# Sums of unmasked banks three units behind their exponentials, and the stretches' limits chosen anew

## The chip, the cores and the metric

The kernel runs on one core of a Trainium2 chip. The time is the device's, in microseconds, from the start of the program to its end; three executions were timed, and one more was profiled. The engines are TensorE (PE, with its weight loads as PEld), VectorE (DVE), ScalarE (ACT), GpSimd (POOL) and SyncE (SP), which issues the DMAs. Each engine works its own list of instructions in order, and semaphores hold one back until another has got far enough.

## The reference

Four layers stand one after the other, on 2048 tokens with 512 features; each adds its result to x.

```python
x = x + _A_ref(_layernorm(x), A_wq, A_wk, A_wv, A_wo, A_beta)   # layer 0
x = x + _B_ref(_layernorm(x), B_wqkv, B_wo)                     # layer 1
x = x + _A_ref(...)                                             # layer 2
x = x + _B_ref(...)                                             # layer 3
```

Layer A has 32 heads of 16 features and four segments of 512 tokens. In a segment it is causal attention (softmax of q·k / 4 under a mask), mixed by a gate for each head with a memory: `num / den`, where `num = phi(q) @ M`, `den = phi(q) @ z`, and `M`, `z` are summed over `phi(k)` and `v` of the segments before. Layer B is plain attention of all 2048 tokens with all, 32 heads, no mask. Both end in a product with `wo`. Nothing in the change touches what is computed.

## The kernel before

A **bank** is one PSUM bank of 128 keys x 512 queries of scores of one head (PSUM has eight). Layer A has masked banks (`k0`, `k13`, `k2`), layer B unmasked ones. A **group** is one head pair's half for one segment of queries: the banks whose exponentials are summed into one sums bank. For each bank three things happen: TensorE makes the scores (`ps<-qm,KB` or `ps<-qm,KA`), an exponential is taken, and TensorE multiplies it with V, extended by a column of ones, which gives numerator and denominator (`pv`, `pv_mm`; these are the "sums").

The exponential has two ways. ACT takes it from PSUM into the ring `pT` (line 1925): two or three banks of a **unit** in one instruction. Or DVE takes it: it turns the scores of a bank into the bits of a bf16 power of two (`dx_first`, line 1394, 16 bits a number), and two shifted copies of those (lines 1450 and 1493 on DVE, line 1475 on POOL, in `task_dx`, `dx_four`, `pool_copy`) are summed with the first, so a bank on DVE costs three products with V in place of one. A unit has three banks for ACT, or two for ACT and one or two for DVE.

The order of all engines' instructions is made by a planner in Python when the program is built (class `Sched` with modelled times, `Builder.attention`). For each unit n it puts into the lists: the scores (`unit`), ACT's exponential, some background work (layer norms, projections, output products, memory; `background`, `bg_one`), and then the sums that are due (`pv_step`). `unit` appends its banks to a first-in, first-out queue `pvq` with the unit in which their sums are due:

```python
entries.append((n + (self.LAG_A if g.kind == "A" else 2), g, what, r, slot, i, width))
```

`pT` has `NPU = 4` slots, used in turn, so what is still queued from unit n-4 is forced out before the exponential of unit n is put down. When a group's last sums are out, `finish` has DVE empty the sums bank (lines 2037 and 2043 for a masked group, line 759 or 2068 to 2072 for an unmasked one, which is written as `ub` in its last part). The next group takes that bank, or the spare one if that comes free earlier (`take_sums`). While the sums bank is late, `attention` puts off the sums of a new group until they are forced.

Whether a bank goes to DVE is decided unit by unit (`dx_open`, `ring_open`, `dx_pick`) by limits, among them: `TAKEN`, the share of a group's banks that DVE may take (`TAKEN_A`, banks of a masked group); `PAIRS`, how many banks must lie ahead for pairs; `PACE`, after how many units without a background task DVE's banks stand back; `POOL_D` and `POOL_C`, how far POOL may be behind DVE and still take the first and the second copy; `FILL` and `keep_busy`, below which share of TensorE's activity products of zeros are put in. The units are cut into 76 **stretches** of 20, and the dictionary `PLAN` gives the limits of each stretch where they differ from the class's own values (`set_limits`). Since each stretch starts from the state that the ones before it left, other limits in one place shift what stands in all later stretches.

Of the kernel before, what the change touches and what calls it, by code (L numbers as in the profile page):

```python
# [416 lines left out]
class Builder:  # L417
# [3 lines left out]
        0: dict(TAKEN_A=1, FILL_DVE=400, MASK_PE=800, PE_LOW=7, GAP=3, QMIN=3, OPART=0, DIV_LATE=2500, PACE=2, DX_LATE=1700, HURRY=1500, POOL_QM=1, POOL_C=0, CR_A=1200, CR_LOW=2000),  # L421
        1: dict(ACT1=300, MARGIN=600, R_LATE=2200, NEAR=5, CR_W=1300, CR_B=1800, R_PAIRS=2, DIV_LATE=2500, TAKEN=0.5, DVE_LATE=800, BG_BANK=100, PHI_LATE=300, OPART=3, NEARW=20, POOL_C=0, DX_LAG=1, POOL_D=2500, REST=8, EARLY=500, POOL_QM=1, DX_FIN=3000, DMA_LATE=1200, TRADE=400, FILL_DVE=400, ORD=13, PACE=12, DMA_STEPS=2, HOLD_AT=12, PE_B=2, TAKEN_A=1, MASK_PE=800, PE_LOW=7, PE_A=4, POOL_MEM=0),
        2: dict(FILL_DVE=400, MASK_PE=800, GAP=3, BG_BANK=400, QMIN=3, LOW=20, POOL_QM=1, ACT1=600, R_PAIRS=2, PE_LOW=7, DX_LATE=1700, DX_FIN=3000, OPART=3, HOLD_AT=12, PE_A=4, NEAR_A=50, TRADE=0, TAKEN_A=1, PART=3, DMA_LATE=700, CR_B=1200, SLACK=350, DMA_STEPS=0, POOL_WAIT=600, MARGIN=250, EVAC_ACT=1500),
# [3 lines left out]
        6: dict(ACT1=300, NEAR=8, TAKEN_A=1, PV_SKIP=900, FILL_DVE=400, BACK=8, CR_W=2200, NEARW=40, OPART=0, TAKEN=0.4, LOW=20, DVE_LATE=800, QWAIT=8, HOLD_AT=40, PHI_LATE=0, REST=20, POOL_D=2500, R_LATE=1200, MARGIN=350, EARLY=300, QUAD=0, CR_A=1700, CARRY_W=1500, PART=3, BUSY_WAIT=500, PE_LOW=7, PE_A=6, HURRY=4000, PAIRS=999, LEVEL=3, DX_BANK=900, DX_LATE=700, QMIN=3, TRADE=400, DVE_LATE_LOW=2500, PACE=7, DVE_FIN=1500, MASK_PE=800, FILL=0.47, DMA_LATE=0),  # L427
        7: dict(R_LATE=1200, NEARW=40, PAIRS=999, MASK_PE=800, LEVEL=3, TAKEN=0.4, LOW=20, MARGIN=350, TAKEN_A=1, EARLY=300, OPART=0, QUAD=0, FILL=0.47, DX_BANK=900, CR_A=1200, DX_LATE=700, CARRY_W=400, PART=3, CR_W=2200, HOLD_MAX=0, DVE_LATE=800, FILL_DVE=400, BUSY_WAIT=500, ACT1=300, DMA_LATE=0, GAP=3, QWAIT=8, NEAR=8, PE_A=6, POOL_QM=1, DVE_LATE_LOW=2500, PACE=7, DVE_FIN=200, HURRY=1500, PV_SKIP=900, POOL_D=2500, PE_LOW=7, QMIN=3),
        8: dict(R_LATE=1200, NEARW=40, PAIRS=999, MASK_PE=800, LEVEL=3, TAKEN=0.4, LOW=30, MARGIN=500, TAKEN_A=1, EARLY=500, OPART=0, QUAD=0, FILL=0.47, DX_BANK=900, CR_A=1200, DX_LATE=700, CARRY_W=1500, PART=3, CR_W=2200, DVE_LATE=1700, FILL_DVE=400, BUSY_WAIT=500, ACT1=300, DMA_LATE=0, QWAIT=8, NEAR=8, PV_SKIP=900, NEAR_A=0, HURRY=1500, QMIN=3),
# [66 lines left out]
        75: dict(DX_LATE=500, REST=8, SLACK=700, R_NEAR=10, R_PAIRS=2, NEARW=90, PAIRS=999, LEVEL=1, LOW=14, GAP=1, QUAD=0, POOL_WAIT=300, PV_SKIP=100, BACK=6, FILL=0.47, PART=0, LN1_AT=3, EARLY=300, DIV_LATE=2500, MARGIN=350, POOL_C=1000, ACT1=300, MASK_PE=200, POOL_D=1200, BUSY_ROOM=300, CR_W=1500, TAKEN=0.5, CR_A=1700, CR_LOW=2000, DX_BANK=700, RATE=2, QWAIT=3, DVE_FIN=1500, POOL_QM=1, DMA_LATE=0),  # L496
# [36 lines left out]
    RUSH, RUSH0 = 0, 0  # L533
# [1832 lines left out]
```

## Time and profile before

| what | us |
|---|---|
| timed executions | 1660.08, 1661.16, 1660.99 (median 1660.99) |
| the profiled execution | 1660.92 |
| its span, first to last instruction | 1659.2 |
| ACT busy | 1622.0 (98%) |
| PE busy | 1573.7 (95%) |
| DVE busy | 1397.2 (84%) |
| POOL busy | 1227.6 (74%) |

PE's busy time is that of pipelined matmuls, and its ends are modelled. A row of a group reads: line, engine, operation, what is written and read, shape, count, then busy time and the mean of one instruction in ns, then the engine's idle time ahead of them and what ended it. A row of the windows reads: from and to, length, then busy time (count) of PE, PEld, DVE, ACT and POOL, the granted clock, DMA share and GB/s; where one line or tile was asked for, only its engine stands there. A row of waits has the total in us, how often, and the longest.

### The profile page before, as it was taken

How to read it: one execution, taken by the hardware profiler on the slowest of the kernel's cores; microseconds unless marked ns; L12 is line 12 of the kernel's file. 1: busy time of each engine (PE TensorE's matmuls, PEld its weight loads, DVE VectorE, ACT ScalarE, POOL GpSimd, SP SyncE). 2: the span in 40 equal slices, each digit the busy share in tenths (PEclk: the TensorE clock that was granted, in tenths of full speed). 3: DMA queues.
4: the chain of work that ended last, by engine and by line, in shares of the span. 5: the costliest groups of instructions: out<-in, count | busy, mean ns of one | idle time of the engine just before them, and what ended most of it. 6: DMA issues, size and time to landing. Idle time of an engine off the chain costs nothing.

```text
span 1659.2 us, 45418 instructions
## 1 busy us (share of the span) xinstructions
PE 1573.7 (95%) x19667; PEld 568.6 (34%) x19738; DVE 1397.2 (84%) x2232; ACT 1622.0 (98%) x1575; POOL 1227.6 (74%) x1322
## 2 busy tenths in 40 slices
PE   8999999999999999999999999999999999999998
PEld 5553435222222535222235222442222222222236
DVE  5668666979998687899878997779899999999996
ACT  7999999999999999999999999999999999999998
POOL 3342234779898443699875898577899999999995
PEclk9999999999999999999999999999999999999999
DMA  6211211001120322200212102112001200100000
GB/s 185 41 21 26 40 27 28 8 8 30 23 62 11 72 68 43 58 11 14 58 24 31 49 14 55 18 21 53 1 14 24 46 11 11 27 11 11 22 16 19
DMA packets 148424, 54.46 MB, mean 33 GB/s; under 512 B 128768, under 2 KB 147712, under 8 KB 148224
## 3 DMA queue, kind: packets, MB, share of 16 engines
q1 hardware_dynamic: 148224, 51.56, 14.8%
q8 instruction: 154, 2.52, 0.7%
q14 instruction: 46, 0.38, 0.1%
HBM read 18.88 MB, written 2.10 MB: 13 GB/s over the span
## 4 chain that ended last, share of the span: by engine, by line
ACT 60%; PE 25%; DVE 9%; DMA 2%; POOL 2%; issue 1%; SPq 0%; ACTq 0%; POOLq 0%
ACT pT L1925 59%; PE ps L683 24%; DVE KA L1394 2%; DVE dxt L1394 1%; ACT amem L966 1%; DVE wA L1394 1%; DVE wB L1394 1%; DMA tb<-ub 1%; DMA xT<-xn 1%; DMA phq<-amem 1%; DMA phk<-KA 0%; SPq L766 0%; POOL pT L1939 0%; DVE lnst L873 0%; DVE xn L895 0%
## 5 line engine op out<-in xcount | busy, mean ns | idle before, releaser
L1925 ACT ACTIVATE pT<-ps 128x1024 bf16<-128x1024 f32 (+1 forms) x1503 | 1592.0, 1230 | 21.0 <-PE ps L683 18.1
L683 PE MATMUL ps<-qm,KB 32*128 32x512 bf16 x4096 | 543.9, 385 | 53.3 <-ACT pT L1925 39.0
L683 PE MATMUL ps<-pT,VB 128*17 128x512 bf16 x2751 | 476.7, 384 | 1.6 <-DVE dxt L1394 0.7
L1475 POOL TENSOR_TENSOR dxt<-dxt,shift 128x512 int32<-128x512 int32 (+1 forms) x293 | 312.8, 1079 | 103.2 <-DVE dxt L1394 73.3
L1394 DVE TENSOR_SCALAR KA<-ps 128x512 uint16<-128x512 f32 (+1 forms) x438 | 339.3, 793 | 24.1 <-PE ps L683 21.7
L683 PEld LDWEIGHTS ps<-qm,KB 32*128 32x128 bf16 x4096 | 139.4, 91 | 558.7 <-ACT pT L1925 442.5
L1394 DVE TENSOR_SCALAR dxt<-ps 128x512 uint16<-128x512 f32 (+1 forms) x332 | 257.3, 789 | 27.3 <-PE ps L683 25.7
L1475 POOL TENSOR_TENSOR QA<-KA,shift 128x512 int32<-128x512 int32 x208 | 227.3, 1103 | 53.4 <-DVE KA L1394 52.9
L683 PE MATMUL ps<-dxt,VB 128*17 128x512 bf16 x1125 | 249.8, 381 | 0.3 <-POOL dxt L1475 0.3
L683 PEld LDWEIGHTS ps<-pT,VB 128*17 128x17 bf16 x2751 | 111.0, 87 | 272.8 <-issue 257.4
L1475 POOL TENSOR_TENSOR VA<-KA,shift 128x512 int32<-128x512 int32 x172 | 184.7, 1083 | 24.0 <-DVE QA L1450 18.5
L1939 POOL TENSOR_SCALAR_AFFINE_SELECT pT<-pT 128x512 bf16<-128x512 bf16 (+4 forms) x135 | 71.7, 546 | 170.7 <-ACT pT L1925 170.4
L1475 POOL TENSOR_TENSOR wA<-wA,shift 128x512 int32<-128x512 int32 (+1 forms) x140 | 151.8, 1096 | 9.8 <-DVE wA L1394 6.4
L683 PE MATMUL ps<-QA,VB 128*17 128x512 bf16 x499 | 145.6, 381 | 0.0
L683 PE MATMUL ps<-VA,VB 128*17 128x512 bf16 x499 | 143.6, 381 | 0.0
L1475 POOL TENSOR_TENSOR wB<-wB,shift 128x512 int32<-128x512 int32 x114 | 124.0, 1102 | 5.9 <-DVE wB L1394 4.3
L683 PE MATMUL ps<-KA,VB 128*17 128x512 bf16 x499 | 127.6, 381 | 0.0
L1394 DVE TENSOR_SCALAR wA<-ps 128x512 uint16<-128x512 f32 (+1 forms) x150 | 120.6, 817 | 8.2 <-PE ps L683 7.3
L683 PE MATMUL ps<-wA,VB 128*17 128x512 bf16 x558 | 125.4, 381 | 0.0
L1394 DVE TENSOR_SCALAR wB<-ps 128x512 uint16<-128x512 f32 (+1 forms) x128 | 103.7, 823 | 4.9 <-PE ps L683 4.7
L683 PE MATMUL ps<-VA,pT 128*128 128x51 bf16 (+1 forms) x2488 | 103.0, 187 | 1.4 <-POOL pT L1939 0.6
L683 PE MATMUL ps<-wB,VB 128*17 128x512 bf16 x471 | 104.2, 381 | 0.0
(174 smaller groups left out, 2061.6 us busy)
## 6 DMA issues: line engine op xcount, KB each, us to landing
wB<-in_B_wqkv_dram SPq DMA_DIRECT2D x48, 128.0 KB, 2.4
wA<-in_A_wk_dram SPq DMA_DIRECT2D x16, 128.0 KB, 2.4
wA<-in_A_wq_dram SPq DMA_DIRECT2D x16, 128.0 KB, 2.6
wA<-in_A_wv_dram SPq DMA_DIRECT2D x16, 128.0 KB, 2.8
out_dram<-x SPq DMA_DIRECT2D x8, 256.0 KB, 2.2
x<-in_A_x_dram SPq DMA_DIRECT2D x3, 512.0 KB, 9.7
wB<-in_B_wqkv_dram SPq DMA_DIRECT2D x1, 1536.0 KB, 12.8
oT<-ob SPq DMA_TRANSPOSE x63, 2.5
```

The source lines that it names most:

```text
L683: self.sc.add("pe", lambda e: e.matmul(out, lhsT, rhs, start=start, stop=stop, skip_group_check=True), reads=reads, banks=[(bank, "w", all ...
L966: self.op("act", lambda e: e.activation(et, src, ACT.Exp), reads=bsrc, writes=self.b_amem, ns=1023, gap=915)
L1394: self.op("dve", lambda e: e.tensor_scalar(d, o, SCALE * LOG2E * 128, 127.0 * 128 + EXP_BIAS, op0=ALU.mult, op1=ALU.add), writes=self.b_dx ...
L1475: self.op("pool", lambda e: e.tensor_tensor(d, s, c, ALU.add), reads=src + [self.b_shift] + [first] * k, writes=dst, ns=165 + 1.75 * n, ga ...
L1925: self.sc.add("act", (lambda dst, src: lambda e: e.activation(dst, src, ACT.Exp, scale=SCALE))(dst, src), writes=self.b_pT[slot * 3 + i:sl ...
L1939: self.op("pool", (lambda blk, pat: lambda e: e.affine_select(blk, blk, pattern=pat, compare_op=ALU.is_ge, fill=0.0, base=0, channel_multi ...
```

## The change

The number of units between an unmasked bank's exponential and its sums becomes a limit `LAG_B`, with 3 as the class's value; stretches 5 and 70 set it to 2. The masked banks keep `LAG_A = 2`. Of the 76 rows of `PLAN`, 54 differ. The code, and two of these rows:

```diff
-    LAG_A = 2
+    LAG_A, LAG_B = 2, 3
...
-            entries.append((n + (self.LAG_A if g.kind == "A" else 2), g, what, r, slot, i, width))
+            entries.append((n + (self.LAG_A if g.kind == "A" else self.LAG_B), g, what, r, slot, i, width))
...
-        4: dict(R_LATE=1200, NEARW=40, PAIRS=999, MASK_PE=800, LEVEL=3, TAKEN=0.5, LOW=20, MARGIN=600, TAKEN_A=1, EARLY=300, OPART=0, QUAD=0, FILL=0.47, DX_BANK=900, CR_A=1200, DX_LATE=700, CARRY_W=1500, PART=3, CR_W=2200, HOLD_MAX=0, DVE_LATE=1700, FILL_DVE=400, BUSY_WAIT=500, ACT1=300, QMIN=3, PE_LOW=7, PE_A=6, TRADE=0, DVE_LATE_LOW=2500, POOL_D=2500, PACE=7, PE_B=6, POOL_MEM=0),
+        4: dict(R_LATE=1200, NEARW=40, PAIRS=999, MASK_PE=800, LEVEL=3, TAKEN=0.5, LOW=20, MARGIN=600, TAKEN_A=1, EARLY=300, OPART=3, QUAD=0, FILL=0.47, CR_A=1200, DX_LATE=700, CARRY_W=1500, PART=3, CR_W=2200, HOLD_MAX=0, DVE_LATE=1700, FILL_DVE=400, BUSY_WAIT=500, ACT1=300, QMIN=3, PE_LOW=7, PE_A=6, TRADE=400, DVE_LATE_LOW=2500, PACE=7, PE_B=6, ORD=3, POOL_WAIT=600),
...
-        5: dict(ACT1=300, NEAR=8, TAKEN_A=1, PV_SKIP=900, FILL_DVE=400, BACK=8, CR_W=2200, NEARW=40, OPART=0, TAKEN=0.4, LOW=20, DVE_LATE=800, QWAIT=8, HOLD_AT=40, PHI_LATE=0, REST=20, POOL_D=2500, R_LATE=1200, MARGIN=350, EARLY=300, QUAD=0, CR_A=1700, CARRY_W=1500, PART=3, BUSY_WAIT=500, PE_LOW=7, PE_A=6, HURRY=4000, PAIRS=999, LEVEL=3, DX_BANK=900, DX_LATE=700, QMIN=3, TRADE=0, DVE_LATE_LOW=2500, PACE=7, DVE_FIN=1500, MASK_PE=800, FILL=0.47),
+        5: dict(ACT1=300, NEAR=8, TAKEN_A=1, PV_SKIP=900, FILL_DVE=400, BACK=8, CR_W=2200, NEARW=40, OPART=0, TAKEN=0.5, LOW=20, DVE_LATE=800, QWAIT=8, HOLD_AT=40, PHI_LATE=0, REST=20, POOL_D=2500, R_LATE=1200, MARGIN=600, EARLY=300, QUAD=0, CR_A=1700, CARRY_W=1500, PART=3, BUSY_WAIT=500, PE_LOW=7, PE_A=6, HURRY=4000, PAIRS=999, LEVEL=3, DX_BANK=900, DX_LATE=700, QMIN=3, TRADE=400, DVE_LATE_LOW=2500, PACE=7, DVE_FIN=1500, MASK_PE=800, FILL=0.47, HOLD_MAX=0, POOL_WAIT=600, LAG_B=2),
```

Of other stretches, what changes in value (a limit that a row does not name has the class's value); some of them have many more edits than are listed:

| stretch | some of its changed limits |
|---|---|
| 9 | none |
| 12, 13 | `TAKEN_A` 0 to 2, `POOL_C` 2000 to 4000, `QMIN` 1 to 4 |
| 16 | `TAKEN` 0.34 to 0.4, `PACE` 12 to 4, `PAIRS` 30 to 60 |
| 22 | `TAKEN` 0.34 to 0.5, `POOL_C` 300 to 4000, `POOL_D` 2500 to 500, `PACE` 0 to 7, `FILL` 0.4 to 0.47 |
| 23 | `PACE` 7 to 2, `FILL` 0.47 to 0.53 |
| 24 | `TAKEN` 0.4 to 0.5, `POOL_C` 300 to 4000, `PACE` 0 to 2 |
| 26 | `PACE` 7 to 2, `RATE` 1 to 2, `QUAD` 0 to 1, `HURRY` 0 to 4000 |
| 32 | `TAKEN` 0.5 to 0.34, `QUAD` 1 to 0, `FILL` 0.55 to 0.47 |
| 33 | `TAKEN` 0.34 to 0.5, `RATE` 1 to 2, `FILL` 0.53 to 0.47 |
| 37 | `PAIRS` 999 to 30, `POOL_C` 300 to 1500, `POOL_D` 1 to 1200, `TAKEN_A` 1 to 0 |
| 54 | `FILL` 0.53 to 0.4, `POOL_D` 500 to 2500, `PAIRS` 30 to 60 |
| 64, 65 | `FILL` 0.53 to 0.4, `EVAC_ACT` 800 to 1500 |
| 66 | `FILL` 0.57 to 0.4, `RATE` 2 to 1 |
| 67, 68 | `FILL` 0.57 to 0.4, `TAKEN` 0.4 to 0.5, `POOL_D` 500 to 2500 |
| 72 | `FILL` 0.53 to 0.4, `TAKEN` 0.5 to 0.4 |

More of the change, by code (lines that the diff above doesn't have):

```diff
@@ L423 @@
-        2: dict(FILL_DVE=400, MASK_PE=800, GAP=3, BG_BANK=400, QMIN=3, LOW=20, POOL_QM=1, ACT1=600, R_PAIRS=2, PE_LOW=7, DX_LATE=1700, DX_FIN=3000, OPART=3, HOLD_AT=12, PE_A=4, NEAR_A=50, TRADE=0, TAKEN_A=1, PART=3, DMA_LATE=700, CR_B=1200, SLACK=350, DMA_STEPS=0, POOL_WAIT=600, MARGIN=250, EVAC_ACT=1500),
+        0: dict(TAKEN_A=1, FILL_DVE=400, MASK_PE=800, PE_LOW=7, GAP=3, QMIN=3, OPART=0, DIV_LATE=2500, PACE=2, DX_LATE=1700, HURRY=1500, POOL_QM=1, POOL_C=0, CR_A=1200, CR_LOW=2000, DVE_FIN=1500, QUAD=0),
@@ new lines @@
+        1: dict(ACT1=300, MARGIN=600, R_LATE=2200, NEAR=5, CR_W=1300, CR_B=1800, R_PAIRS=2, DIV_LATE=2500, TAKEN=0.5, DVE_LATE=800, BG_BANK=100, PHI_LATE=300, OPART=3, NEARW=20, POOL_C=0, DX_LAG=1, POOL_D=2500, REST=8, EARLY=500, POOL_QM=1, DX_FIN=3000, DMA_LATE=1200, TRADE=400, FILL_DVE=400, ORD=13, PACE=12, DMA_STEPS=2, HOLD_AT=12, PE_B=2, TAKEN_A=1, MASK_PE=800, PE_LOW=7, PE_A=4, POOL_MEM=0, FILL=0.53),
+        2: dict(FILL_DVE=400, MASK_PE=800, GAP=3, BG_BANK=400, QMIN=3, LOW=20, POOL_QM=1, ACT1=600, R_PAIRS=2, PE_LOW=7, DX_LATE=1700, DX_FIN=3000, OPART=0, HOLD_AT=12, PE_A=4, NEAR_A=50, TRADE=0, TAKEN_A=1, PART=3, DMA_LATE=700, CR_B=1200, SLACK=350, DMA_STEPS=0, POOL_WAIT=600, MARGIN=400, EVAC_ACT=1500),
@@ new lines @@
+        13: dict(MARGIN=600, NEAR=10, PV_SKIP=200, FILL_DVE=400, BUSY_ROOM=300, FILL=0.53, CR_W=1500, CARRY_W=400, R_PAIRS=2, GAP=3, DVE_LATE=800, QMIN=4, POOL_QM=1, PAIRS=999, SLACK=350, R_NEAR=10, CR_B=1800, QWAIT=8, LN1_AT=6, CR_A=1200, POOL_D=2500, POOL_WAIT=0, POOL_C=4000, PACE=7, MASK_PE=800, ACT1=300, RATE=2, REST_A=20, CR_LOW=4000, PART=0, LEVEL=3, BG_BANK=100, QUAD=0, R_LATE=1500, PE_A=4, SPARE=20, EARLY=500, DVE_FIN=1500, TAKEN_A=2),
+        14: dict(EVAC_ACT=100, NEAR=5, SLACK=350, R_NEAR=10, CARRY_W=400, NEARW=90, OPART=4, PAIRS=60, DIV_LATE=2500, TAKEN=0.4, DVE_LATE=1700, BUSY_BACK=800, CR_W=2200, POOL_C=2000, DX_LATE=900, REST=12, PV_SKIP=100, BUSY_ROOM=900, FILL=0.4, R_PAIRS=2, DX_LAG=1, QWAIT=3, QMIN=1, LOW=30, POOL_D=2500, ORD=3, PORT_FREE=150, FILL_DVE=400, GAP=1, ACT1=300, REST_A=20, DMA_STEPS=0, DVE_LATE_LOW=9000, TAKEN_A=1, PACE=4),
@@ new lines @@
+        21: dict(MARGIN=500, NEAR=10, PV_SKIP=100, FILL_DVE=100, BUSY_ROOM=300, FILL=0.4, CR_W=1300, CARRY_W=400, R_PAIRS=2, OPART=4, GAP=1, DVE_LATE=800, QMIN=1, HOLD_AT=40, POOL_QM=1, ACT1=300, DX_LATE=900, REST=8, CR_B=1800, DX_LAG=1, BACK=6, LOW=14, BUSY_WAIT=500, POOL_D=2500, PART=0, PHI_LATE=0, EVAC_ACT=1500, RUSH0=40, HURRY=1500, AHEAD=1000, ORD=3, PORT_FREE=900, DMA_STEPS=0, PE_B=6, DMA_LATE=0, QUAD=0, POOL_MEM=4000),
+        22: dict(ACT1=300, DX_LATE=500, NEAR=10, PV_SKIP=200, EARLY=300, FILL=0.47, CR_B=1800, CARRY_W=1500, OPART=0, MASK_PE=800, DIV_LATE=800, BG_BANK=100, QUAD=0, LN1_AT=6, FILL_DVE=400, R_LATE=1500, POOL_C=4000, QMIN=4, POOL_D=500, DVE_LATE=1700, DX_FIN=3000, POOL_QM=1, DVE_FIN=1500, MARGIN=500, PACE=7, DX_BANK=700, LEVEL=3, TAKEN=0.5, PART=3, CR_W=2200, HOLD_MAX=0, BUSY_WAIT=500, PE_LOW=7, PE_A=6, TRADE=400, DVE_LATE_LOW=2500, QWAIT=8, SLACK=350, GAP=1, NEARW=90, CR_A=1200),
@@ new lines @@
+        43: dict(ACT1=300, MARGIN=400, R_LATE=2200, EVAC_ACT=800, NEAR=5, CR_W=1300, CR_B=1800, R_PAIRS=2, DIV_LATE=800, TAKEN=0.5, DVE_LATE=800, BG_BANK=100, PHI_LATE=300, OPART=3, NEARW=20, POOL_C=4000, DX_LAG=1, POOL_D=2500, REST=12, EARLY=500, POOL_QM=1, DX_FIN=3000, DMA_LATE=700, PE_LOW=7, PACE=7, AHEAD=100, CR_A=1700, DVE_FIN=200, HOLD_MAX=0, DX_LATE=700, GAP=1, CR_LOW=4000, BUSY_ROOM=900, PORT_FREE=900, POOL_WAIT=600),
+        44: dict(ACT1=300, MARGIN=400, R_LATE=2200, EVAC_ACT=800, NEAR=5, CR_W=1300, CR_B=1800, R_PAIRS=2, DIV_LATE=2500, TAKEN=0.5, DVE_LATE=800, BG_BANK=100, PHI_LATE=300, OPART=3, NEARW=20, POOL_C=4000, DX_LAG=1, POOL_D=2500, REST=12, EARLY=500, POOL_QM=1, DX_FIN=3000, DMA_LATE=700, PE_LOW=7, PACE=7, AHEAD=100, CR_A=1700, DVE_FIN=200, HOLD_MAX=0, DX_LATE=700, GAP=1, CR_LOW=4000, BUSY_ROOM=900, PORT_FREE=900, POOL_WAIT=600, FILL_DVE=100, DVE_LATE_LOW=2500),
@@ new lines @@
+        47: dict(ACT1=300, MARGIN=600, R_LATE=1200, EVAC_ACT=800, NEAR=10, CR_W=1300, CR_B=1800, R_PAIRS=2, DIV_LATE=2500, TAKEN=0.5, DVE_LATE=800, BG_BANK=100, PHI_LATE=300, OPART=3, NEARW=20, POOL_C=1000, DX_LAG=1, POOL_D=2500, REST=12, EARLY=500, POOL_QM=1, DX_FIN=3000, DMA_LATE=1200, PE_LOW=7, PORT_FREE=900, TRADE=400, RATE=2, DX_LATE=700, FILL=0.53, CARRY_W=1500, LN1_AT=6, FILL_DVE=400, POOL_WAIT=0, BUSY_ROOM=300, RUSH=40, TAKEN_A=2, SPARE=60),
+        48: dict(ACT1=200, DX_LATE=700, NEAR=10, PV_SKIP=200, EARLY=500, FILL=0.47, CR_B=1800, CARRY_W=1500, OPART=2, MASK_PE=200, DIV_LATE=800, DVE_LATE=800, BG_BANK=100, QUAD=0, FILL_DVE=400, R_LATE=2200, POOL_C=2000, BACK=8, RUSH0=40, MARGIN=600, PE_B=6, DMA_LATE=700, QMIN=4, DX_FIN=3000, SLACK=250, HURRY=2500, TRADE=0, POOL_QM=1, FIT=3, TAKEN_A=5, DMA_STEPS=2),
@@ L479 @@
[L479 removed]
+        57: dict(R_LATE=1500, DX_LATE=700, REST=12, TAKEN_A=1, R_NEAR=50, PV_SKIP=500, FILL_DVE=400, BUSY_ROOM=900, CR_W=1300, DX_LAG=1, LOW=20, HOLD_SEGS=2, BACK=8, R_PAIRS=2, BG_BANK=100, EVAC_ACT=100, EARLY=500, CR_A=1200, POOL_QM=1, POOL_D=1200, DVE_LATE=1700, POOL_C=4000, PORT_FREE=900, PART=0, RUSH0=40, ORD=-7),
@@ L497 @@
+        75: dict(TAKEN_A=2, RUSH=120, POOL_C=2000),
     }
```

90 lines of the change are left out of this document (39 added, 51 removed).

## The prediction, before the changed kernel was run

> **What bounds the kernel now.** I read the page first (engines, slices, chain), then the groups by form, then windows cut at the planner's stretches. One unit issues one exponential, so stretch k runs from exponential 20k to 20k+19, and its window follows from their starts.
>
> ```profile
> span 1659.2 us, 45418 instructions
> PE 1573.7 (95%) x19667; PEld 568.6 (34%) x19738; DVE 1397.2 (84%) x2232; ACT 1622.0 (98%) x1575; POOL 1227.6 (74%) x1322
> ...
> DVE  5668666979998687899878997779899999999996
> ACT  7999999999999999999999999999999999999998
> POOL 3342234779898443699875898577899999999995
> ...
> ACT 60%; PE 25%; DVE 9%; DMA 2%; POOL 2%; issue 1%; SPq 0%; ACTq 0%; POOLq 0%
> ...
> L683 PE MATMUL ps<-qm,KB 32*128 32x512 bf16 x4096 | 543.9, 385 | 53.3 <-ACT pT L1925 39.0
> L683 PE MATMUL ps<-pT,VB 128*17 128x512 bf16 x2751 | 476.7, 384 | 1.6 <-DVE dxt L1394 0.7
> ```
>
> ACT is the bound: 1622.0 of 1659.2 us. The slices show two halves: at the end ACT, DVE and POOL are all at 9, and in the first half DVE and POOL have slices of 3 to 7. The same by windows (us, then busy time of PE, PEld, DVE, ACT, POOL):
>
> ```profile
> 44.74:313.72 268.98, 253.20 (x3548) 117.66 (x3575) 187.62 (x372) 261.78 (x225) 107.08 (x153) 0.99 0.16 28
> ...
> 518.62:689.62 171.00, 163.44 (x2383) 74.25 (x2396) 127.36 (x241) 169.01 (x155) 85.44 (x110) 1.00 0.25 49
> ...
> 1099.12:1627.22 528.10, 505.38 (x5601) 141.48 (x5594) 504.95 (x701) 525.97 (x544) 501.11 (x482) 1.00 0.09 20
> ```
>
> From 1099 to 1627 us ACT is idle for 2.1 us, DVE for 23.2 (4%), POOL for 27.0 (5%): nothing to shift there but crumbs. In the first two windows together DVE is idle for 81.4 + 43.6 = 125.0 us and POOL for 247 us, while ACT is full. So time can be won in two ways only: ACT's idle time, or banks that go from ACT to DVE and POOL in the first two thirds. ACT's idle time at the two ends is not up for change:
>
> ```profile
> 0.00:44.74 44.74, 38.80 (x586) 23.99 (x594) 24.52 (x60) 34.10 (x34) 17.11 (x41) 1.00 0.59 172
> 1647.12:1659.20 12.08, 7.84 (x141) 4.90 (x140) 2.26 (x5) 5.60 (x7) 0.00 (x0) 0.96 0.13 45
> ```
>
> 10.6 us go at the start and 6.5 at the end, of 37.2 in all; 20.1 us are left between them.
>
> **The price of a bank.** ACT takes two banks in one instruction, or three where DVE takes none:
>
> ```profile
> L1925 ACT ACTIVATE pT<-ps 128x1024 bf16<-128x1024 f32 x1050 | 1004.6, 1110 | 9.6 <-PE ps L683 7.8
> L1925 ACT ACTIVATE pT<-ps 128x1536 bf16<-128x1536 f32 x453 | 649.1, 1508 | 11.4 <-PE ps L683 10.3
> ```
>
> They overlap, so I take busy time over count: 1004.6 / 1050 = 0.957 us and 649.1 / 453 = 1.433 us. A bank that DVE takes out of a unit of three saves ACT 0.476 us. It costs DVE its first step, and two shifted copies, which POOL makes for two banks at a time:
>
> ```profile
> L1394 DVE TENSOR_SCALAR KA<-ps 128x512 uint16<-128x512 f32 x347 | 231.6, 681 | 16.2 <-PE ps L683 14.6
> ...
> L1475 POOL TENSOR_TENSOR QA<-KA,shift 128x512 int32<-128x512 int32 x208 | 227.3, 1103 | 53.4 <-DVE KA L1394 52.9
> ```
>
> So 0.681 us of DVE and, for two copies of half of 1.103, 1.1 us of POOL.
>
> **Part 1, the lag.** Sums of unmasked (layer 1 and 3) banks of unit n are put into TensorE's order in unit n+3 in place of n+2. No instruction is added. Can it remove a wait? The sums that read pT wait for 1.6 us in the whole span (their row above): two units behind, they are never late, since the scores of unit n already wait for the exponential of unit n-2 to free their PSUM banks. Direct gain: 0 to 1.6 us; I take 0. What it gives otherwise is one more unit in which a group's DVE banks can become ready; what it takes is a unit of the ring of four pT slots, so that at a change of groups the next group's sums can be put off by one unit at most (by two before) while DVE still empties the PSUM bank of the last one. I take 0 for this, and price it as a rival. Where masked banks stand behind unmasked ones, the queue is first in, first out, so one unit issues two units' sums. That lump lies in TensorE's wait of 39.0 us for ACT where TensorE is ahead. Without that cover it costs:
>
> ```profile
> L683 PE MATMUL ps<-VA,pT 128*128 128x51 bf16 x2296 | 101.8, 188 | 1.2 <-POOL pT L1939 0.6 <-DVE x L1228 0.3
> ...
> L683 PE MATMUL ps<-VB,pT 128*128 128x51 bf16 x279 | 14.4, 187 | 0.0
> ```
>
> Three banks are 12 matmuls of 101.8 / 2296 = 0.044 us, 0.53 us, at most once for each of 32 pairs of masked groups. The chain has PE for 25% and ACT for 60%, so PE leads in 25/85 = 0.29 of the places: 32 x 0.53 x 0.29 = 4.9 us as the upper end, 0 taken. At the very end of the kernel one more unit's sums stand behind the last exponential: two banks, 8 matmuls of 14.4 / 279 = 0.052, 0.4 us; half lies in waits there already, so **+0.2 us**.
>
> **Part 2, the limits.** 54 of 76 stretches change. Most edits have no price of their own, since they decide which task is put into an order. Those that admit more or fewer banks to DVE have one. Wider, in stretches with idle DVE: 5 and 24 (share of a group that DVE may take 0.4 to 0.5), 22 (0.34 to 0.5), 37 (pairs from 30 banks ahead in place of 999, POOL's copies on in place of nearly off). The windows of 5, 22, 24, 37, and then DVE's first steps (line 1394) in the same four:
>
> ```profile
> 159.29:189.42 30.13, 28.49 (x355) 13.66 (x352) 17.10 (x36) 30.13 (x29) 3.00 (x7) 1.00 0.31 52
> 539.46:566.67 27.21, 25.68 (x438) 16.01 (x442) 18.58 (x37) 26.40 (x22) 14.61 (x19) 1.00 0.54 99
> 591.38:614.66 23.28, 21.95 (x277) 7.20 (x274) 19.27 (x38) 23.28 (x23) 6.44 (x7) 1.00 0.34 81
> 877.38:904.34 26.96, 23.57 (x471) 15.80 (x472) 23.80 (x49) 24.65 (x24) 17.40 (x27) 1.00 0.17 27
> ```
>
> ```profile
> 159.29:189.42 30.13, 1.38 (x2) 1.00 0.31 52
> 539.46:566.67 27.21, 4.74 (x7) 1.00 0.54 99
> 591.38:614.66 23.28, 5.87 (x10) 1.00 0.34 81
> 877.38:904.34 26.96, 7.18 (x11) 1.00 0.17 27
> ```
>
> DVE is idle there for 13.0, 8.6, 4.0 and 3.2 us. The smallest holds 3.2 / 0.681 = 4 first steps, and POOL has the 4.4 us for the copies in each (27.1, 12.6, 16.8, 9.6 idle). I take 4 banks for each of the four: 16 x 0.476 = **-7.6 us**. Lower end: none, if another limit binds (scores wait for a PSUM bank, a group too near its end). Upper end: an eighth of the 125.0 idle us of DVE, 15.6 / 0.681 = 22 banks, -10.5 us. Narrower: 23 (after 2 units in place of 7 without a background task, DVE's banks wait for it) and 32 (share 0.5 to 0.34).
>
> ```profile
> 566.67:591.38 24.71, 5.63 (x9) 1.00 0.23 50
> 770.37:790.09 19.72, 13.12 (x19) 1.00 0.06 15
> ```
>
> Of these 28 first steps I estimate one in ten lost: 3 x 0.476 = **+1.4 us**; lower end 0, upper end a third of them, 9 x 0.476 = 4.3. The edits from 54 on work where DVE, POOL and ACT are full (third window): 0, and at most the 23.2 idle us of DVE at one part in five, 7 banks or 3.3 us either way. Where ACT idles between the ends, a gap that goes may come back elsewhere once the order is new; I take 0 of the 20.1 us.
>
> **Sum.** -7.6 + 1.4 + 0.2 = -6.0 us. The profiled execution took 1660.92 us by itself, 1.7 around its span, and the median is 1660.99: the two agree to 0.1. Forecast **1655.0 us**.
>
> **Rivals.**
>
> A, more than forecast (1650.7): an eighth of DVE's idle time in the first two windows is used, 10.5 us with the 0.2. For it: POOL stands at 107.08 of 268.98 us. Against: layer 0's masked banks bring at most one bank of a group to DVE, and most stretches there keep their limits.
>
> B, no change (1661.2): the limits named do not bind, the shares are reached by other conditions, and the lag alone changes nothing. For it: first steps in stretch 5 number 2, far from any share. Against: in 24 DVE idles for 4.0 us and ACT for none, so each bank that is admitted there shortens the bound.
>
> C, **slower** (1665.1): late sums banks. At every end of an unmasked group DVE empties the bank that the next group's sums need.
>
> ```profile
> L766 SPq DMA_TRANSPOSE tb<-ub x62: 1189/1190/1383, 383.2 to 1613.8; - x62
> ...
> L759 DVE CAST ub<-ps x36: 658/681/692, 477.6 to 1613.1; 128x512 bf16<-128x512 f32 x36
> ```
>
> At least 62 such ends, 0.681 us each, on a DVE that is 96% busy after 1099 us. With one unit of put-off left, TensorE (in order) waits, with the next scores behind it, and ACT behind those. In full and where PE leads: 62 x 0.681 x 0.29 = 12.2 us; where ACT leads, the rest beyond TensorE's own pause before scores hides. If five in six ends wait so, 10.1 us come on the forecast's 1655.0. It decides (past 1664.3) from 9.3 / 12.2 = three quarters of them on. Against: PE waits on group ends hardly at all now, and the planner may put a new group into the other spare bank.
>
> D, the clock: the fill threshold goes from 0.57 to 0.4 in stretches 64 to 68 (in 64 and 65 from 0.53). Before, the granted clock fell once between the ends (windows; the clock is the third number from the end):
>
> ```profile
> 276.00:280.00 4.00, 3.20 (x59) 2.10 (x58) 2.47 (x5) 3.84 (x3) 3.11 (x4) 1.00 0.42 83
> 280.00:284.00 4.00, 3.15 (x56) 2.22 (x57) 2.85 (x5) 2.45 (x3) 3.02 (x4) 0.82 0.27 56
> 284.00:288.00 4.00, 3.77 (x43) 1.54 (x45) 2.33 (x5) 2.76 (x3) 3.67 (x6) 0.75 0.00 0
> ```
>
> The longest wait of PE in these 12 us, from the view of waits:
>
> ```profile
> PE ps L683 <- POOL qm L1802: 1.4, 1, 1.4
> ```
>
> ACT lost 8.00 - 5.21 = 2.8 us there. Two more such drops give 1655.0 + 5.6 = 1660.6, four 1666. Against: no drop in the dense windows. The Trainium skill (TensorE: Matmul & The Clock Gate, HAM oscillation) has the rule that the throttle needs a pause of the array above some 3.4 us; here it came with PE busy for 3.20 and 3.15 of 4 us and a longest wait of 1.4 us. By that rule D could not happen and its chance would go to the forecast; the row decides.
>
> **Chances.** Forecast 0.41, A 0.15, B 0.20, C 0.15, D 0.09. A run of this kind tells a difference from 0.2%, 3.3 us, so 1657.7 and 1664.3 are the bounds. Faster: 0.33 of the forecast's share, A's 0.15, 0.02 of B and 0.01 of D, 0.51. Within: 0.07, 0.12 of B, 0.05 of D and 0.03 of C, 0.27. Slower: 0.12 of C, 0.06 of B, 0.03 of D, 0.01 of the forecast, 0.22. The range leaves out half of A's spread below (A at its upper end with a gap of stretch 37 gone, 1648) and C's end above (all ends waiting, 1667): **1648 to 1666**. The forecast's own: 1651 to 1659.
>
> **What would show it.** Right: more first steps on line 1394 in all and fewer exponentials of 128x1536, ACT's busy time down by 5 to 7 us, its idle time within 3 us of 37.2. Part 1: the idle time before the sums that read pT stays near 1.6 us. C: PE waits for DVE's ub or ob grow past 5 us, and ACT's idle with them. D: more windows with a clock under 1. Wrong altogether: ACT's busy time unchanged or up, or a gain between 1099 and 1627 us above 3.3.

## The result: slower by 9.8 us

The changed kernel takes 1670.75 us (median; 1670.16 to 1673.48) against 1660.99. The ratio, taken over all executions, is 1.0065, with a 95% interval of 1.0042 to 1.0087. The forecast was 1655.0, and the range ended at 1666.

The page of the kernel after, with the engines, three rows of the slices, the chain and two groups:

```profile
span 1669.0 us, 45126 instructions
PE 1577.7 (95%) x19541; PEld 570.0 (34%) x19616; DVE 1377.9 (83%) x2154; ACT 1635.2 (98%) x1575; POOL 1231.4 (74%) x1353
...
DVE  5666676878998687899777997778989999999995
ACT  7999999999999999999999999999999999999998
POOL 3343224779888554799765898566999999999996
...
ACT 66%; PE 23%; DVE 6%; POOL 2%; issue 2%; DMA 1%; ACTq 0%; DVEq 0%; POOLq 0%
...
L683 PE MATMUL ps<-qm,KB 32*128 32x512 bf16 x4096 | 542.6, 385 | 58.9 <-ACT pT L1925 43.4
L683 PE MATMUL ps<-pT,VB 128*17 128x512 bf16 x2771 | 479.6, 385 | 3.0 <-DVE wB L1394 1.0
```

ACT is still the bound, and more so: 66% of the chain in place of 60%. Its busy time went from 1622.0 to 1635.2, **+13.2 us**, and its idle time (span less busy) from 37.2 to 33.8, **-3.4 us**. The two make the whole 9.8 us. DVE's busy time fell by 19.3. So work went from DVE to ACT. The groups by form say which:

```profile
L1925 ACT ACTIVATE pT<-ps 128x1024 bf16<-128x1024 f32 x1016 | 971.6, 1088 | 6.8 <-PE ps L683 5.0
L1925 ACT ACTIVATE pT<-ps 128x1536 bf16<-128x1536 f32 x485 | 690.0, 1496 | 11.4 <-PE ps L683 10.2
```

Units of three banks went from 453 to 485. ACT now takes 2 x 1016 + 3 x 485 = 3487 banks, against 2 x 1050 + 3 x 453 = 3459 before: 28 more, so DVE takes 28 fewer. At the prediction's price of 0.476 us these are 13.3 us; ACT's busy time grew by 13.2 (12.5 of them in line 1925: 1592.0 to 1604.5 us).

**Where.** I cut both runs at the same work, between the starts of the 2305th score product of an unmasked bank (1108.0 us before, 1111.9 after) and the last one (1649.2 and 1659.3). The windows of that part, before and then after (columns as in the prediction):

```profile
1108.00:1649.20 541.20, 518.42 (x6025) 154.71 (x6023) 512.60 (x715) 538.85 (x556) 507.98 (x486) 1.00 0.09 19
```

```profile
1111.90:1659.30 547.40, 519.53 (x6006) 156.94 (x6008) 502.33 (x680) 545.09 (x554) 509.16 (x493) 1.00 0.09 19
```

6.2 of the 9.8 us are lost here, where I had called DVE, POOL and ACT full and had put 0. ACT is busy 6.2 us longer, DVE 10.3 us less: its idle time went from 28.6 to 45.1 us. Another 3.9 us are lost before 1111.9, and 0.3 come back after the last product. Of the 3.9, 3.4 are there when stretch 12 starts (336.1 us before, 339.5 after), and a drop of TensorE's clock at 129 us has 2.9 us in that: the changed kernel with another limit in stretch 12 (e6), whose instructions are the same up to there, hasn't the drop and starts the stretch at 336.6. The kernel before has a shorter drop in that part, of 0.9 to 1.4 us (last section).

The stretches that the prediction named, by DVE's first steps (line 1394) in their windows after: 5, 22, 24, 37, then 23 and 32, and two that it didn't name, 34 and 74.

```profile
163.73:193.91 30.18, 1.38 (x2) 1.00 0.26 54
541.89:567.92 26.03, 6.00 (x8) 1.00 0.42 104
592.60:615.69 23.09, 6.78 (x10) 1.00 0.41 99
880.34:906.24 25.90, 7.85 (x10) 1.00 0.16 23
567.92:592.60 24.68, 4.04 (x6) 1.00 0.23 33
771.17:791.00 19.83, 14.32 (x16) 1.00 0.04 7
811.26:834.98 23.72, 7.51 (x9) 1.00 0.26 60
1637.31:1660.02 22.71, 8.59 (x13) 1.00 0.02 4
```

34 and 74 before:

```profile
810.60:831.94 21.34, 11.79 (x16) 1.00 0.17 33
1627.22:1647.12 19.90, 11.90 (x18) 1.00 0.01 4
```

DVE's time in first steps rose by 0, 1.3, 0.9 and 0.7 us in the four stretches with wider limits: 2.8 us, some 4 banks and not 16. In 23 and 32 it fell by 1.6 and rose by 1.2. And in stretch 34 it fell by 4.3, in 74 by 3.3, two of many with edits that I had priced at nothing.

### The profile page after: what moved, and what is told of

Read it like the earlier page. It is cut to its first block, busy times and chain, and to the rows that moved or that the text cites. A ratio compares the mean times of both kernels' runs of the same rounds, so it can differ in the third digit from the quotient of the medians.

```text
span 1669.0 us, 45126 instructions
## 1 busy us (share of the span) xinstructions
PE 1577.7 (95%) x19541; PEld 570.0 (34%) x19616; DVE 1377.9 (83%) x2154; ACT 1635.2 (98%) x1575; POOL 1231.4 (74%) x1353
## 4 chain that ended last, share of the span: by engine, by line
ACT 66%; PE 23%; DVE 6%; POOL 2%; issue 2%; DMA 1%; ACTq 0%; DVEq 0%; POOLq 0%
ACT pT L1925 65%; PE ps L683 23%; DVE dxt L1394 1%; DVE wB L1394 1%; ACT amem L966 1%; DVE KA L1394 1%; POOL dxt L1475 1%; DMA phq<-amem 0%; POOL wA L1475 0%; DVE dxt L1450 0%; POOL pT L1939 0%; DVE x L1228 0%; DVE lnst L873 0%; POOL VA L1475 0%; DMA phk<-KA 0%
## 5 line engine op out<-in xcount | busy, mean ns | idle before, releaser
L1925 ACT ACTIVATE pT<-ps 128x1024 bf16<-128x1024 f32 (+1 forms) x1501 | 1604.5, 1219 | 18.2 <-PE ps L683 15.2
L1475 POOL TENSOR_TENSOR dxt<-dxt,shift 128x512 int32<-128x512 int32 (+1 forms) x311 | 326.5, 1062 | 86.8 <-DVE dxt L1394 45.5
L1394 DVE TENSOR_SCALAR KA<-ps 128x512 uint16<-128x512 f32 (+1 forms) x407 | 326.1, 821 | 37.3 <-PE ps L683 34.7
L1475 POOL TENSOR_TENSOR QA<-KA,shift 128x512 int32<-128x512 int32 (+1 forms) x220 | 241.6, 1109 | 69.5 <-DVE KA L1394 69.3
L1939 POOL TENSOR_SCALAR_AFFINE_SELECT pT<-pT 128x256 bf16<-128x256 bf16 (+4 forms) x155 | 80.1, 532 | 174.8 <-ACT pT L1925 174.5
L1475 POOL TENSOR_TENSOR wB<-wB,shift 128x512 int32<-128x512 int32 (+1 forms) x112 | 121.4, 1098 | 15.3 <-DVE wB L1394 13.4
L1475 POOL TENSOR_TENSOR wA<-wA,shift 128x512 int32<-128x512 int32 x107 | 115.8, 1098 | 3.2 <-DVE wA L1394 2.3
L1394 DVE TENSOR_SCALAR wA<-ps 128x512 uint16<-128x512 f32 (+1 forms) x129 | 102.6, 811 | 6.1 <-PE ps L683 5.5
L683 PE MATMUL ps<-VA,pT 128*128 128x34 bf16 (+1 forms) x2512 | 104.0, 187 | 1.2 <-DVE ob L2043 0.3
L683 PE MATMUL ps<-qm,KA 32*128 32x128 bf16 (+2 forms) x1536 | 92.8, 254 | 8.9 <-ACT pT L1925 4.1
```

Of the source, the lines that this page charges most:

```text
L683: self.sc.add("pe", lambda e: e.matmul(out, lhsT, rhs, start=start, stop=stop, skip_group_check=True), reads=reads, banks=[(bank, "w", all ...
L1394: self.op("dve", lambda e: e.tensor_scalar(d, o, SCALE * LOG2E * 128, 127.0 * 128 + EXP_BIAS, op0=ALU.mult, op1=ALU.add), writes=self.b_dx ...
L1475: self.op("pool", lambda e: e.tensor_tensor(d, s, c, ALU.add), reads=src + [self.b_shift] + [first] * k, writes=dst, ns=165 + 1.75 * n, ga ...
L1925: self.sc.add("act", (lambda dst, src: lambda e: e.activation(dst, src, ACT.Exp, scale=SCALE))(dst, src), writes=self.b_pT[slot * 3 + i:sl ...
L1939: self.op("pool", (lambda blk, pat: lambda e: e.affine_select(blk, blk, pattern=pat, compare_op=ALU.is_ge, fill=0.0, base=0, channel_multi ...
```

## The experiments

Two theories. **F, the fit:** a set of limits serves the one order that it was chosen with, and in any other order the same limits admit fewer banks and let more waits in. Then no edit has a price by its own meaning. **C, the lag's own price:** rival C of the prediction, late sums banks. All times are medians, and ratios are to the kernel before, run beside them. The times that the expectations of e1 to e4 name under F count lost banks alone.

### The two parts, one at a time

Old limits with the new lag (e1):

```diff
-    LAG_A = 2
+    LAG_A, LAG_B = 2, 3
...
-            entries.append((n + (self.LAG_A if g.kind == "A" else 2), g, what, r, slot, i, width))
+            entries.append((n + (self.LAG_A if g.kind == "A" else self.LAG_B), g, what, r, slot, i, width))
```

with `LAG_B=2` in stretches 5 and 70, as in the change.

> The limits of before with the new lag (3, and 2 in stretches 5 and 70). The program gives 1235 banks to DVE, 42 fewer than before. Theory F (limits fit one order; any other order loses DVE banks, the lag has no price of its own): 42 x 0.476 = 20 us of ACT, so about 1681 us, and the new limits are what brings the changed kernel back to 1671. Theory L (the new lag costs by itself and the new limits are neutral): the same 1671 as the changed kernel. Theory N (the new limits cost, the lag is neutral): 1661.

New limits with the old lag (e2), against the changed kernel:

```diff
-    LAG_A, LAG_B = 2, 3
+    LAG_A, LAG_B = 2, 2
```

> The limits of after with the old lag 2 in all stretches. 1247 banks go to DVE, 30 fewer than before. Theory F: 30 x 0.476 = 14 us, about 1675 us, slower than the changed kernel, since these limits belong to the order with lag 3. Theory L: back to before, 1661. Theory N: the changed kernel's 1671.

| us | two units behind | three units behind |
|---|---|---|
| old limits | 1660.99 | 1731.94 (1.0431, 1.0413 to 1.0448) |
| new limits | 1694.90 (1.0211, 1.0196 to 1.0226) | 1670.75 |

Neither part is small. The lag alone costs 71 us, the limits alone 34, and together they cost 9.8. They can't be added. F's estimates, 1681 and 1675 us, fall short by 51 and 20 us: more is lost than banks. From the pages of e1 and of e2:

```profile
span 1730.9 us, 45471 instructions
...
PE 1617.1 (93%) x19728; PEld 579.0 (33%) x19801; DVE 1379.1 (80%) x2144; ACT 1651.5 (95%) x1575; POOL 1221.6 (71%) x1331
...
L683 PE MATMUL ps<-pT,VB 128*17 128x512 bf16 x2796 | 481.3, 385 | 10.2 <-DVE wA L2068 2.2
```

```profile
span 1695.9 us, 45114 instructions
...
PE 1594.5 (94%) x19536; PEld 570.6 (34%) x19611; DVE 1378.2 (81%) x2144; ACT 1641.8 (97%) x1579; POOL 1237.4 (73%) x1347
...
L683 PE MATMUL ps<-pT,VB 128*17 128x512 bf16 x2774 | 476.8, 385 | 2.9 <-DVE KA L2068 1.0
```

In e1 ACT is busy 29.5 us longer than before and idle for 79.4 us in place of 37.2. TensorE's idle time ahead of the sums that read `pT` is 10.2 us; the largest part that the page names, 2.2 us, was released by DVE's emptying of a sums bank (line 2068). With the lag of two (e2) the idle time is 2.9 us. That row speaks for C, the rest for F.

### A number that means next to nothing

If F holds, a small edit to a limit must cost as much. `MARGIN` is how many ns the planner wants TensorE ahead of ACT before it gives it a background task. The kernel before, with 700 in place of 600 in one stretch of 76 (e3); the same edit in the changed kernel (e6); and in the kernel before a late edit, the fill threshold of one stretch (e4):

```diff
-        12: dict(MARGIN=600, ...
+        12: dict(MARGIN=700, ...
```

```diff
-        54: dict(..., FILL=0.53, ...
+        54: dict(..., FILL=0.58, ...
```

> The kernel before with one limit of one stretch moved a little: MARGIN 600 to 700 in stretch 12 (background work waits for 0.1 us more spare time on TensorE). 1241 banks go to DVE, 36 fewer. Theory F: an edit that means nothing costs as much as the whole change or more: 36 x 0.476 = 17 us, 1678 us. Theories L and N: within 0.2% of before, 1658 to 1664, as the edit touches neither the lag nor the limits that they blame.

> The kernel before with one limit of a late stretch moved: FILL 0.53 to 0.58 in stretch 54. Up to 1236 us the program is that of before. 1264 banks go to DVE, 13 fewer. Theory F: 13 x 0.476 = 6 us, 1667 us: a late nudge costs less, as fewer stretches are left whose limits no longer fit. Theories L and N: 1661.

> The changed kernel with one limit moved: MARGIN 600 to 700 in stretch 12, the same nudge as in the kernel before. 1242 banks go to DVE, 7 fewer than in the changed kernel. Theory F: the changed kernel is fitted to its own order as the one before is to its own, so it loses some 25 to 45 us, 1695 to 1715. If instead the changed kernel were as it is because of the lag alone: 1671 within 4 us.

Measured: e3 1703.41 us (1.0263, 1.0248 to 1.0279), e4 1674.56 (1.0087, 1.0072 to 1.0103), e6 1711.51 (1.0307, 1.0291 to 1.0322), which is 40.8 us over the changed kernel. The engines of e3:

```profile
PE 1601.3 (94%) x19627; PEld 577.2 (34%) x19700; DVE 1378.2 (81%) x2169; ACT 1644.4 (97%) x1578; POOL 1235.8 (73%) x1346
```

With a span of 1701.2, ACT is busy 22.4 us longer and idle 19.6 us longer than before, from one number in one stretch. F's estimates by banks alone, 1678 and 1667 us for e3 and e4, are again too low, and e6 lies within its 1695 to 1715. The loss is not at the place of the edit alone: the 1025th score product of an unmasked bank starts 18 us later in e3 than before (at 553.1 us), the 2305th 24 us later, the last one 42. So F holds as far as these runs go: both kernels stand on limits that fit their own order, and leaving the fit costs some 40 us where 63 stretches follow and 14 where 21 follow. All nudges raise a limit; lowering one was not tried. Against such losses, the 9.8 us of the change read as the difference between two fits. The trace of before can't show this: nothing in it tells a limit that fits from one that doesn't.

### The lag only in the last third

Old limits, and three units behind from stretch 54 on (e5):

```diff
-        54: dict(..., POOL_MEM=0),
+        54: dict(..., POOL_MEM=0, LAG_B=3),
```

and so on to 75, with `LAG_B = 2` as the class's value.

> The limits of before, lag 2 up to stretch 53 and lag 3 from 54 on; up to 1236 us the program is that of before. 1270 banks go to DVE, 7 fewer than before; the nudge in the same stretch 54 had 13 fewer and 1674.6 us. Theory F (limits fit one order, the lag is only one more way to leave it): 1661 to 1675, not slower than that nudge. Theory C (lag 3 also costs by itself, as sums wait for a sums bank that DVE has not emptied): over 1680, and TensorE's idle time before sums that read pT grows by 5 us or more.

1681.76 us (1.0134, 1.0119 to 1.0149): 7.2 more than the nudge at the same place (e4), though DVE took 6 more banks than there. ACT's idle time is 53.0 us against e4's 41.7. TensorE's idle time ahead of the `pT` sums, for which C had 5 us more than before, rose from 1.6 to 3.8 only (2.5 in e4). A price of the lag by itself, beside the lost fit, is likely; it needs pairs.

### Four pairs with equal limits

To part C from F, neither lag should have the fit. The class's own values in all stretches (e7 with two units, e8 with three):

```diff
-    PLAN = {
-        0: dict(TAKEN_A=1, ...
...
-    }
+    PLAN = {}
```

the new limits with the nudge in stretch 12 at two units (e9, against e6), the old ones with that nudge at three (e10, against e3), and the old ones with `MARGIN` 350 in place of 250 in stretch 2 at both (e11, e12).

> All stretches with the class's own limits, lag 2: limits fitted to no order in particular. 1134 banks go to DVE, 143 fewer than before: 143 x 0.476 = 68 us and TensorE's lateness as in the nudges, 20 to 60 more: 1750 to 1790. It is the partner of the next run.

> As the run before with lag 3; 1130 banks go to DVE. Neither order is favoured by the limits here. Theory F: the same as with lag 2 within 10 us. Theory C: slower than with lag 2 by 15 us or more, TensorE's idle time before sums that read pT 5 us or more above that with lag 2.

> The partner of the nudged changed kernel: the new limits with MARGIN 600 to 700 in stretch 12, lag 2 everywhere. 1232 banks go to DVE, 10 fewer than with lag 3. Theory C (lag 3 costs some 20 us by itself where neither order is favoured, as with the class's limits): 1685 to 1700, faster than the 1711.5 with lag 3 in spite of fewer banks on DVE, and TensorE idle before sums that read pT for 1 to 3 us, not 8.5. Theory F alone (lag of no price): 1711 plus 5 to 12 for the banks, 1715 to 1725.

> The partner of the nudge in stretch 12: the limits of before with MARGIN 700 there, lag 3 (2 in stretches 5 and 70). 1249 banks go to DVE, 8 more than with lag 2. Theory C: 1720 to 1735, idle time of TensorE before sums that read pT 7 us or more (2.7 with lag 2). Theory F alone: 1694 to 1704.

> A second nudge of the kernel before, in another place: MARGIN 250 to 350 in stretch 2, lag 2. 1241 banks go to DVE, as with the nudge in stretch 12. Both theories: 1695 to 1710 like that one, since an early nudge leaves nearly all stretches with limits that no longer fit.

> The same nudge in stretch 2 with lag 3 (2 in stretches 5 and 70). 1248 banks go to DVE, 7 more than with lag 2. Theory C: 15 us or more above its partner, idle time before sums that read pT of 7 us or more. Theory F alone: 3 to 9 us below its partner.

| limits | two | three | more | ACT busy | ACT idle | PE idle ahead of the `pT` sums |
|---|---|---|---|---|---|---|
| class's (e7, e8) | 1762.04 | 1782.02 | 20.0 | +1.6 | +19.2 | 1.0 to 7.0 |
| new, nudged in 12 (e9, e6) | 1702.42 | 1711.51 | 9.1 | -4.3 | +12.2 | 2.3 to 8.5 |
| old, nudged in 12 (e3, e10) | 1703.41 | 1724.63 | 21.2 | +2.6 | +19.0 | 2.7 to 12.5 |
| old, nudged in 2 (e11, e12) | 1710.64 | 1746.27 | 35.6 | +2.7 | +32.8 | 3.0 to 8.6 |

The ratios to before are 1.0616 (1.06 to 1.0631) and 1.0734 (1.0716 to 1.0752) for the first pair; 1.0261 (1.0246 to 1.0276) for e9; 1.0389 (1.0374 to 1.0405) for e10; 1.0308 (1.0291 to 1.0325) and 1.0525 (1.0509 to 1.0541) for the last pair. Four of four are slower with three units, by 9 to 36 us, as C expected in all but a detail: e9 is 2.4 us above its range. ACT's work hardly differs. What grows is ACT's idle time, and TensorE's wait ahead of the sums with it. The rows of e3 and of e10:

```profile
L683 PE MATMUL ps<-pT,VB 128*17 128x512 bf16 x2794 | 474.4, 384 | 2.7 <-DVE wB L1394 0.7 <-DVE dxt L1394 0.7 <-DVE x L1228 0.5
```

```profile
L1925 ACT ACTIVATE pT<-ps 128x1536 bf16<-128x1536 f32 x485 | 690.3, 1486 | 31.4 <-PE ps L683 30.1
...
L683 PE MATMUL ps<-pT,VB 128*17 128x512 bf16 x2786 | 483.6, 385 | 12.5 <-DVE ub L2072 2.1 <-DVE dxt L1394 1.9 <-DVE wA L1394 1.8
```

TensorE stands before the sums for DVE: by the releasers that the trace infers: a group's end (`ub`, line 2072), and first steps on line 1394, which read a bank that sums can go into. ACT's wait for scores of three banks is 30.1 us, against 21.5 in e3. In e8 the clock fell at two places more than in e7, with 2.2 of the 19.2 us.

The pairs that are nudged in stretch 12 are not clean ahead of it, where the limits still fit the order of one lag. I cut them at the 385th score product of an unmasked bank, which stands in stretch 11 in all four. e10 reaches it 11.9 us after e3 (2.9 of them by a drop of the clock, last section) and loses 9.7 behind it, where ACT's idle time goes from 40.1 to 49.4 us. e6 reaches it 0.5 us ahead of e9 and loses 8.5 behind it. The windows from there to the end, of e3, of e10 and of e14 (which comes below):

```profile
326.70:1701.20 1374.50, 1297.06 (x15325) 432.10 (x15362) 1152.43 (x1714) 1334.36 (x1307) 1103.20 (x1145) 1.00 0.13 28
338.60:1722.80 1384.20, 1309.16 (x15478) 434.05 (x15478) 1157.62 (x1726) 1334.84 (x1307) 1100.06 (x1139) 1.00 0.13 28
351.60:1737.20 1385.60, 1307.41 (x15440) 437.28 (x15473) 1153.23 (x1710) 1335.41 (x1308) 1095.89 (x1130) 1.00 0.13 28
```

So C holds too, as a price of the lag where no order is favoured: 8.5, 9.7, 20.0 and 35.6 us. The size is loose, since a lag is a nudge too, and e3 and e11, which differ by the place of a nudge alone, are 7 us apart.

### One unit of put-off, with two units behind

C says that the lag costs because a new group's sums can then be put off by one unit only, since `pT` has four slots. These kernels take that unit away and leave the lag at two (e13 with the class's limits, e14 and e15 with the old ones nudged in 12 and in 2):

```diff
-        while any(e[4] == slot for e in self.pvq):
+        while any(e[4] == slot or e[1].kind == "B" and e[0] < n for e in self.pvq):
             self.cr_dve -= self.pv_step(n)
```

> Class limits in all stretches, sums two units behind, but a new group's unmasked sums may be put off by one unit only, as three units behind leaves it with four pT slots. Theory 'put-off' (the price of three units behind is the lost unit of put-off): the time goes to that of class limits with three units, 1782, within 6, and TensorE's idle time before the sums that read pT rises from 1.0 to 5 us or more. Theory 'place' (the price lies in the later place of the sums itself, in lumps and the group's later end): it stays at 1762 within 6, with 1 to 2 us there. Between 1768 and 1776 both have a part.

> The kernel before with MARGIN 700 in stretch 12, two units behind, put-off of one unit at most. Against 1703.4 with two units of put-off and 1724.6 with three units behind. Theory 'put-off': 1724.6 within 8, sums' idle 8 us or more. Theory 'place': 1703.4 within 8, sums' idle 2 to 4 us.

> The kernel before with MARGIN 350 in stretch 2, two units behind, put-off of one unit at most. Against 1710.6 with two units of put-off and 1746.3 with three units behind. Theory 'put-off': 1746 within 12, sums' idle 7 us or more. Theory 'place': 1710.6 within 8, sums' idle 2 to 4 us.

| limits | two units of put-off | one | more | ACT busy | ACT idle | PE idle ahead of the `pT` sums |
|---|---|---|---|---|---|---|
| class's (e7, e13) | 1762.04 | 1773.91 (1.0689, 1.0673 to 1.0705) | 11.9 | -1.8 | +12.9 | 1.0 to 6.0 |
| old, nudged in 12 (e3, e14) | 1703.41 | 1738.53 (1.0477, 1.0459 to 1.0494) | 35.1 | +1.2 | +34.8 | 2.7 to 11.2 |
| old, nudged in 2 (e11, e15) | 1710.64 | 1737.74 (1.0474, 1.0458 to 1.0489) | 27.1 | +18.0 | +9.5 | 3.0 to 12.1 |

The row of e14:

```profile
L683 PE MATMUL ps<-pT,VB 128*17 128x512 bf16 x2777 | 478.7, 384 | 11.2 <-DVE x L1228 2.4 <-DVE ub L759 2.2 <-DVE KB L2068 1.3
```

In all three the wait ahead of the sums comes back at two units behind, about as large as at three (6.0, 11.2 and 12.1 us against 7.0, 12.5 and 8.6). That the lost unit of put-off makes this wait is shown. How much of the time it makes is not settled: e15 lies within what theory 'put-off' expected, e13 between the two theories, e14 above both. In e15 most of the loss is ACT's work: DVE has 42 banks fewer than in e11, 20 us by the price of a bank. In e13 TensorE's clock fell at five places in place of one (windows of 2 us with a clock below 1, the kernel's end apart), and 7.3 of its 12.9 us of idle ACT lie there. Only e14 has neither. It lost more than three units behind did (1738.5 against 1724.6), but 24.9 us of the loss are there at the 385th product (351.6 us against e3's 326.7), where e3 still has the fit of the kernel before. Behind it e14 loses 11.1 us and three units behind 9.7 (the windows above). So in the one pair where neither DVE's banks nor the clock differ, the lost unit of put-off costs about as much as the lag. Waits of TensorE ahead of the sums, 5 to 9 us more, are also less than what ACT loses; through what the rest goes, I didn't follow.

## Why the prediction was wrong

**The price of a bank held.** 28 banks at 0.476 us are 13.3, and ACT's busy time grew by 13.2.

**Part 2 failed in its method.** I priced an edit by its own meaning: wider share, more banks. The four wider stretches brought 2.8 us of first steps where 16 banks would have been 10.9, and the sum over all stretches went the other way, 28 banks fewer. A wider limit lets a bank through only where the others let it too, as rival B had it of stretch 5 (2 first steps before and after). e3 shows why the sign of an edit says nothing here: 100 ns in one stretch cost 42 us.

**0 from stretch 54 on, with at most "7 banks or 3.3 us either way"**, missed by 6.2 us; the stretches ahead of it, with -6.2 forecast and 3.9 lost, by 10.1. The 3.3 us took DVE's 23.2 idle us for all that could change there. The fullness was no property of the work but of the fit: with another order DVE idled 16.5 us more by the same work, and 6.2 us were lost. In e4 one limit of stretch 54 costs 13.6 us.

**Part 1's 0 for the lag** was wrong in its own terms. That the sums "are never late" held for two units of put-off, and the pairs give 8.5 to 35.6 us for three units behind. Rival C named the mechanism and the place; its 12.2 us at most were within that spread, but it multiplied group ends by DVE's 0.681 us, and the runs show DVE's first steps in the spare bank among what TensorE waits for as well. In the changed kernel itself C doesn't show as a wait: 3.0 us ahead of the sums, against 1.6, and ACT's idle time is down by 3.4. The new limits avoid the waits (41.8 to 15.2 us of ACT waiting for scores between e6 and the changed kernel, which differ by the nudge alone). They have 28 banks fewer on DVE. Whether they had to give up those banks to avoid the waits is argued, not shown.

**What would have shown it** worked: "wrong altogether: ACT's busy time unchanged or up". **D** didn't come about as more drops: the clock fell once between the ends in both, at 282 us before and at 129 us after, in a stretch that the change gave no lower fill threshold. The later one is twice as long and cost 2.9 us, against 0.9 to 1.4 for the one before (last section). The prediction's 2.8 us took all of ACT's idle time there for the drop's; in the same 8 us e4, with the same instructions and no drop, idled for 1.8. The execution of the changed kernel in which the granted clock shows no such loss (1.0) took 1670.16 us, so the drop doesn't make the result.

**The range** failed because both unknown parts were bounded by idle time seen in one trace. The bound for a new order is what an unfitted order costs, and one nudged kernel would have shown that it is some 40 us.

## What to carry to other kernels

Where a planner's limits were chosen for one order, a change of the order and the choice of new limits are one experiment: the 2 x 2 table (1661, 1732, 1695, 1671) shows that neither part has a price that can be read from one pair of its times. Before such an edit is costed from a trace, ask what a meaningless edit of the same kind costs; if that is more than the effect in question, the trace of one kernel can't give the sign. And to learn what a structural change is worth, compare both structures under several settings that favour neither.

## What the hardware showed unasked

With the same instructions, a drop of TensorE's clock comes in one execution and not in another. The windows of the changed kernel (granted clock third from the end), and the longest wait of TensorE from 116 to 132 us, in the view of waits:

```profile
124.00:128.00 4.00, 3.51 (x54) 1.39 (x51) 0.94 (x3) 4.00 (x4) 1.43 (x3) 1.00 0.00 0
128.00:132.00 4.00, 3.24 (x25) 0.71 (x21) 2.62 (x5) 3.68 (x4) 0.00 (x0) 0.67 0.02 3
132.00:136.00 4.00, 4.00 (x31) 0.98 (x28) 1.38 (x2) 1.74 (x2) 0.00 (x0) 0.50 0.60 64
```

```profile
PE ps L683 <- ACT pT L1925: 1.3, 3, 0.6
```

The same windows of e6, whose instructions on ACT, DVE and POOL are those of the changed kernel for 340 us:

```profile
124.00:128.00 4.00, 3.51 (x54) 1.38 (x51) 0.94 (x3) 4.00 (x5) 1.34 (x3) 1.00 0.00 0
128.00:132.00 4.00, 3.24 (x37) 1.09 (x33) 3.22 (x6) 4.00 (x4) 0.00 (x0) 1.00 0.04 9
132.00:136.00 4.00, 3.83 (x47) 1.21 (x44) 3.42 (x6) 3.88 (x5) 0.00 (x0) 1.00 0.62 61
```

TensorE is busy for the same 3.51 and 3.24 us, and the clock stays at 1. e10 and e12, which also run three units behind there, have the drop at 128 as the changed kernel has; e1, with the instructions of e10 up to 355 us, has none there. e3, e4 and e5 have those of the kernel before past 282 us, and none has its drop. Only e7, e8 and e13, alike up to 135 us, all have one at 26. So the place of a drop doesn't follow from the instructions alone; what else decides it stays open.

Such pairs also give the price of a drop. The clock time lost was near 1.7 us in most drops and near 3.4 in the others, as in this one. When stretch 12 starts, the changed kernel is 2.9 us behind e6, and e10 is 2.9 behind e1; the kernel before, with its drop of 1.7, is 0.9 to 1.4 behind e3, e4 and e5. ACT was idle here for 0.32 + 2.26 = 2.6 of the 8 us, and for 0.1 in e6. Besides the rule on long pauses that the prediction held against such drops, the Trainium skill (TensorE: Matmul & The Clock Gate, A second HAM failure mode: psum-queue depth-cycling) tells of a clock that falls where TensorE has frequent short pauses between groups of matmuls. Here the pauses were few (three waits, 1.3 us in 16, none above 0.6), and up to 129 us e6 had the same two waits without a drop, so this case doesn't bear that out.
